# Float64 weights made float32 two chunks at a time: tiles of 2 x 512 columns, two heads' inputs to a tile

## The chip, the cores and the metric

One core of a Trainium2 chip runs the whole program. Its engines each work through a queue of their own in order: TensorE (PE, with its weight loads as PEld), VectorE (DVE), ScalarE (ACT) and GpSimd (POOL); SyncE (SP) issues the DMA transfers. The metric is the device time of one execution in microseconds (us), smaller is better. The kernel before takes 1027.05 us, the median of three runs (1026.56 to 1028.83).

## What is computed

Three layers follow each other: causal attention with a decay bias, and two feed-forward layers without routing, cut to what matters:

```python
# q, k, v: (4, 8, 576, 64)   s: (4, 8, 576)   out: (4 * 576, 512)
def attn(q, k, v, s):
    cum = cumsum(maximum(s, 0), -1)
    scores = q @ k.T / 8 + minimum(-(cum[..., :, None] - cum[..., None, :]), 0)
    p = exp(causal(scores) - rowmax)
    return (p / (p.sum(-1) + 1e-9)) @ v
x = attn(q, k, v, s) as (2304, 512)
h = x @ w1_in               # (512, 2048)
x = (h * clip(h + 3, 0, 6) / 6) @ w1_out
h = x @ w2_in
out = (h * sigmoid(h)) @ w2_out
```

The four weight matrices, of 512 x 2048 or 2048 x 512, are float64: their spreads 1 / sqrt(512) and 1 / sqrt(2048) are float64 scalars by which the float32 draws are multiplied. The chip gets them as pairs of 32-bit words, low word first, and makes float32 values of them with shifts, masks and an addition on integers. The products are then computed with each operand split into a high part (fp32r) and a low part, as high x high + high x low + low x high.

## The kernel before

The attention has 64 heads, 32 of part A (query rows 0 to 255) and 32 of part B (rows 256 to 575), in the order "A0 A1 A2 B0 A3 B1 B2 B3" of part and batch with eight heads each. The first feed-forward layer works on eight blocks of tokens of the same order, each over 16 chunks f of 128 hidden rows; a chunk of the input weights (`W["i", 0, f]`) and one of the output weights (`W["o", 0, f]`) is 128 x 512 values. The second layer works on three blocks of 768 tokens over eight pairs q of chunks.

The loop over slots (L785 on) drives the first part. A slot holds the scores of one head, the second half of the head before it, and, from the tenth slot on, one step of the first layer: `first` (L239 to L241: x times the input weights into the PSUM tile ph), `gate_high` (L251 on ScalarE, L252 on VectorE, then the high part gh) and `gate_low` (L259), and one step later `second` (L278 to L280: into the accumulators acc). In the first block a step is one chunk f, on 256 tokens. The next step's `first` reuses the only ph bank and so needs L252 of the step before.

A chunk of weights (class `Chunk`, L115) lives in one tile of `wpool`, with the tag `i0` to `i15` or `o0` to `o15`. `load` (L132) brings 512 KB of words. `fields` on ScalarE scales the low words (L144) and the high words (L145, into a tile `mag` of the pool `stage`, three buffers). `join` on VectorE is three instructions (L153 sign, L157 shift, L160 addition); `high` (L105, by `copy`) writes the high part into the chunk's own tile, `low` (L171) the low part. `Feed.tick` (L184) takes each chunk through these in turn: load, three ticks later `fields`, one later `join`, one later `high` and `low`. In the trace the tile of the words is rawi or rawo, that of the parts wi or wo, `mag` is magi or mago.

The first feed has the 32 chunks of the first layer. `ticks(3)` (L775) loads three ahead of the slots, between the loads of heads 0 and 1 and the loads of their bias rows (L398, L399); the slots add 0.4 tick each up to the ninth and two each from the tenth (L796). The first 14 heads have their inputs (inA) in the tiles of the chunks that are loaded late (`spare`, L344: one tile to a head); `srow` and `crow` and the rows of `split_rows` lie in tiles `i7`, `o7`, `i15`, `o15`, `i6` and `o6`.

The second layer's input weights go by class `Two` (L843): two chunks at a time are converted with `Chunk`'s instructions, four sums are made of them (L871), and all is split into high and low in a tile w (L881, L883), of which there are two. Its output weights go by a second feed of 16 chunks, ticked by `outs2` (L903): in the last block of the first layer from its ninth step, then twice per pair q. Both take their `mag` tiles from `stage`, and so do three of the four output tiles of `finish1` for the last block (L669).

All this is program order. A scheduler that simulates the engines turns it into the order of each engine's queue: it takes the instruction that stands first in the program among those that are ready at its simulated time. So work is often drawn far ahead, and the order is fixed by the simulated times and not by those on the chip.

Of the kernel before, what the change touches and what calls it, by code (L numbers as in the profile page):

```python
# [27 lines left out]
def kernel(  # L28
# [36 lines left out]
    stage = ctx.enter_context(tc.tile_pool(name="stage", bufs=3))  # L65
# [49 lines left out]
    class Chunk:  # L115
        def __init__(self, kind, m, f):
            self.key = (kind, m, f)
            self.src = ((w1i, w1o), (w2i, w2o))[m][kind == "o"][f]
            self.nm = f"{kind}{m}_{f}"
            self.home = wpool, f"{kind}{f}"  # L120

        def place(self, shape, dt, name):
            pool, tag = self.home
            return pool.tile(shape, dt, tag=tag, name=f"{name}{self.nm}")
# [38 lines left out]
        def high(self, eng):  # L163
            wt = self.place([P, 2, DM], F32R, "w")
            W[self.key] = wt[:, 0, :], wt[:, 1, :]
            copy(eng, W[self.key][0], self.val)

        def low(self, eng):
            hi, lo = W[self.key]
            e = nc.vector if eng == "v" else nc.gpsimd  # L170
            e.tensor_tensor(out=lo, in0=self.val, in1=f32(hi), op=ALU.subtract)  # L171

    class Feed:


        def __init__(self, keys, hi_eng, lo_eng):
            self.ch = [Chunk(*k) for k in keys]
            self.hi_eng, self.lo_eng = hi_eng, lo_eng
# [64 lines left out]
    def gate_high(i):  # L243
# [3 lines left out]
        g = gpool.tile(sh, F32, tag="g", name=f"g{i}")  # L247
# [64 lines left out]
    def bank(kind, shape, name):  # L312
# [7 lines left out]
        wpool.tile([BH, S], F32, tag=f"{kd}{NF // 2 - 1}", name=f"{kd}row") for kd in "io"  # L320
# [7 lines left out]
    def split_rows():  # L328

        def row(tag, name):  # L330
            return wpool.tile([BH, S], F32R, tag=tag, name=name)

        f = NF - 1
        hi, lo = row(f"i{f}", "cumh"), row(f"o{f}", "cuml")
        one, neg = row(f"i{NF // 2 - 2}", "one"), row(f"o{NF // 2 - 2}", "neg")
# [8 lines left out]
    spare = [f"{kd}{f}" for f in range(NF // 2, NF) for kd in "io"][:14]  # L344

    class Head:
# [322 lines left out]
    def finish1(blk, accs):  # L669
        n = sizes[blk][1]  # L670
        per = 512 // n
        for i, c in enumerate(range(0, NDC, per)):
            pool, tag = (gpool, "g") if blk < NB1 - 1 else (stage, "mag") if i else (w7pool, "s4")
            o = pool.tile([P, per, n], F32, tag=tag, name=f"o{blk}_{c}")
# [10 lines left out]
    feed = Feed([(kd, 0, f) for f in range(NF) for kd in "io"], "a", "v")  # L685
# [89 lines left out]
    ticks(3)  # L775
# [8 lines left out]
    for has_head, has_step in plan:  # L784
# [10 lines left out]
        if not feed.done():  # L795
            rate = ((0.4,)*9+(2,))[min(nslot, len(((0.4,)*9+(2,))) - 1)]  # L796
# [98 lines left out]
    feed = Feed([("o", 1, f) for f in range(NF)], "a", "v")  # L895
# [7 lines left out]
    def outs2(upto):  # L903

        while feed.t < min(upto, NF + 5):
# [15 lines left out]
    def split2(b):  # L921
# [5 lines left out]
        def parts(name, x):  # L927
            n0 = 2 + 2 * ["b11", "b22", "t2", "b21", "t3", "t1", "t4"].index(name)
            xh, xl = [
                wpool.tile([P, 2, TH], F32R, tag=f"i{n0 + k}", name=f"x{k}{name}_{b}")  # L930
                for k in range(2)
            ]
# [244 lines left out]
```

## Time and profile before

| | |
|---|---|
| median of 3 runs | 1027.05 us (1026.56 to 1028.83) |
| the profiled execution | 1026.95 us, span 1025.2 us |
| PE busy in the span | 988.9 us (96%) |
| DVE busy | 720.5 us (70%) |
| ACT busy | 523.5 us (51%) |
| chain that ended last | PE 84%, DVE 7%, DMA 5%, SP's queue 3% |
| DMA | 124.78 MB, mean 122 GB/s |

The span is the time from the first to the last instruction of the profiled execution; 1.75 us lie around it. A busy matmul is not one at its peak: its end is modelled and overlaps the next one, so the distance of two starts is the better measure of what one costs. The same holds for instructions that follow each other on VectorE and ScalarE. The chain is followed back from the last instruction to what released each step.

### The profile page before, as it was taken

What the parts mean: (1) busy time and instruction counts of PE and PEld (TensorE: products, weight loads), DVE (VectorE), ACT (ScalarE), POOL (GpSimd) and SP (SyncE); (2) the same over time, 40 slices, a digit from 0 to 9 for tenths busy, and PEclk for the clock granted to TensorE, in tenths of its full rate; (3) what the DMA queues carried; (4) which work ended last, traced back from release to release, by engine and by line L of the source; (5) the groups of instructions that cost most, each with busy time, mean ns of one, the idle gap of its engine ahead of it and who ended that gap; (6) DMA issues with size and microseconds to landing.
All of it is one profiled execution on the core that took longest, in us unless ns stands there. A gap on an engine that the chain in (4) does not pass through costs nothing.

```text
span 1025.2 us, 18219 instructions
## 1 busy us (share of the span) xinstructions
PE 988.9 (96%) x6322; PEld 918.1 (90%) x6322; DVE 720.5 (70%) x1797; ACT 523.5 (51%) x1141; POOL 205.6 (20%) x378
## 2 busy tenths in 40 slices
PE   4978999999999999999999999899999999999997
PEld 3878899999999999999998888789888899888996
DVE  6699996788778887887737997977574343743343
ACT  5697854555455666665515563755353232532232
POOL 5000133443244444444411131000000000000000
PEclk9999999999999999999999999999999999999999
DMA  5794131122312222222113975443345332433411
GB/s 152 208 316 151 49 94 44 51 79 54 90 56 69 85 65 69 86 65 68 58 43 106 350 284 196 143 163 136 144 154 185 144 127 90 165 135 122 144 72 62
DMA packets 52067, 124.78 MB, mean 122 GB/s; under 512 B 10004, under 2 KB 31752, under 8 KB 48648
## 3 DMA queue, kind: packets, MB, share of 16 engines
q1 hardware_dynamic: 51528, 122.97, 35.9%
q8 instruction: 50, 0.82, 0.3%
q10 hardware_dynamic: 448, 0.66, 0.2%
q14 instruction: 41, 0.34, 0.1%
HBM read 98.96 MB, written 24.63 MB: 121 GB/s over the span
## 4 chain that ended last, share of the span: by engine, by line
PE 84%; DVE 7%; DMA 5%; SPq 3%; issue 1%; ACT 1%; DVEq 0%; ACTq 0%
PE ph L239 6%; PE ph L241 6%; PE ph L240 6%; PE acc L279 6%; PE acc L280 6%; PE acc L278 6%; PE a L985 6%; PE a L987 6%; PE a L986 6%; PE h L969 5%; PE h L971 5%; PE h L970 5%; PE poB L595 4%; PE pt0B L546 1%; PE pt1B L546 1%; DMA rawi<-in_w1i_dram 1%
## 5 line engine op out<-in xcount | busy, mean ns | idle before, releaser
L239 PE MATMUL ph<-xh,wi 128*128 128x256 f32 (+1 forms) x512 | 155.0, 304 | 9.0 <-DVE g L252 8.9
L279 PE MATMUL acc<-gl,wo 128*128 128x256 f32 (+1 forms) x512 | 153.2, 301 | 0.8 <-DVE gl L259 0.7
L240 PE MATMUL ph<-xl,wi 128*128 128x256 f32 (+1 forms) x512 | 152.7, 298 | 0.0
L241 PE MATMUL ph<-xh,wi 128*128 128x256 f32 (+1 forms) x512 | 152.4, 298 | 0.0
L280 PE MATMUL acc<-gh,wo 128*128 128x256 f32 (+1 forms) x512 | 151.2, 297 | 0.0
L278 PE MATMUL acc<-gh,wo 128*128 128x256 f32 (+1 forms) x512 | 145.9, 301 | 0.2 <-DVE gh L107 0.2
L1027 ACT ACTIVATE gh<-h 128x384 fp32r<-128x384 f32 x96 | 50.3, 524 | 180.1 <-DVE h L1035 179.8
L985 PE MATMUL a<-wo,gh 128*128 128x512 f32 x288 | 113.0, 392 | 2.2 <-ACT gh L1027 2.2
L986 PE MATMUL a<-wo,gh 128*128 128x512 f32 x288 | 113.0, 392 | 0.0
L239 PEld LDWEIGHTS ph<-xh,wi 128*128 128x128 f32 x512 | 98.0, 192 | 14.0 <-DVE g L252 9.4
L279 PEld LDWEIGHTS acc<-gl,wo 128*128 128x128 f32 x512 | 96.8, 189 | 5.5 <-DVE gl L259 2.2
L240 PEld LDWEIGHTS ph<-xl,wi 128*128 128x128 f32 x512 | 98.3, 192 | 2.9
L241 PEld LDWEIGHTS ph<-xh,wi 128*128 128x128 f32 x512 | 98.1, 192 | 2.8
L280 PEld LDWEIGHTS acc<-gh,wo 128*128 128x128 f32 x512 | 96.6, 189 | 3.7
L278 PEld LDWEIGHTS acc<-gh,wo 128*128 128x128 f32 x512 | 95.8, 189 | 4.5 <-DVE gh L107 0.6
L987 PE MATMUL a<-wo,gl 128*128 128x512 f32 x288 | 89.6, 393 | 0.5 <-DVE gl L1029 0.5
L251 ACT ACTIVATE g<-ph,half 128x512 f32<-128x512 f32 (+1 forms) x80 | 51.3, 644 | 64.7 <-PE ph L241 64.0
L1029 DVE TENSOR_TENSOR gl<-h,gh 128x384 fp32r<-128x384 f32 x96 | 53.4, 556 | 40.6 <-ACT h L1028 38.8
L252 DVE SCALAR_TENSOR_TENSOR g<-g,ph 128x512 f32<-128x512 f32 (+1 forms) x80 | 50.2, 629 | 39.9 <-ACT g L251 39.5
L1035 DVE TENSOR_TENSOR h<-h,u 128x384 f32<-128x384 f32 x72 | 40.1, 557 | 54.0 <-PE h L971 53.7
L99 POOL TENSOR_SCALAR gh<-g 128x512 fp32r<-128x512 f32 x64 | 51.1, 798 | 125.4 <-DVE g L252 113.3
L969 PE MATMUL h<-x0t,w 128*128 128x384 f32 x192 | 65.1, 339 | 0.7 <-DVE u L1035 0.7
(224 smaller groups left out, 2553.3 us busy)
## 6 DMA issues: line engine op xcount, KB each, us to landing
w<-w_d SPq DMA_DIRECT2D x18, 1792.0 KB
w_d<-w SPq DMA_DIRECT2D x8, 1792.0 KB
k2B<-in_kT_dram SPq DMA_DIRECT2D x64, 144.0 KB
rawi<-in_w1i_dram SPq DMA_DIRECT2D x16, 512.0 KB
rawo<-in_w1o_dram SPq DMA_DIRECT2D x16, 512.0 KB
rawi<-in_w2i_dram SPq DMA_DIRECT2D x16, 512.0 KB
rawo<-in_w2o_dram SPq DMA_DIRECT2D x16, 512.0 KB
q2B<-in_qT_dram SPq DMA_DIRECT2D x64, 80.0 KB
```

The lines of the kernel that those rows point to most:

```text
L239: nc.tensor.matmul(o, wih[:, cs], xh[c], start=c == 0, stop=False)
L240: nc.tensor.matmul(o, wih[:, cs], xl[c], start=False, stop=False)
L241: nc.tensor.matmul(o, wil[:, cs], xh[c], start=False, stop=c == NDC - 1)
L251: nc.scalar.activation(g, ph, AF.Relu, bias=half, scale=1.0 / 6.0)
L278: nc.tensor.matmul(a, woh[:, cs], gh[:, jj, :], start=b0, stop=False)
L279: nc.tensor.matmul(a, woh[:, cs], gl[:, jj, :], start=False, stop=False)
L280: nc.tensor.matmul(a, wol[:, cs], gh[:, jj, :], start=False, stop=b1)
L969: nc.tensor.matmul(ps, w[:, 0, cs], xh[:, c, :], start=c == 0, stop=False)
L985: nc.tensor.matmul(accs[t], gh[:, k, cs], woh, start=b0, stop=False)
L986: nc.tensor.matmul(accs[t], gh[:, k, cs], wol, start=False, stop=False)
L987: nc.tensor.matmul(accs[t], gl[:, k, cs], woh, start=False, stop=b1)
L1029: nc.vector.tensor_tensor(out=gl[:, i, o], in0=g, in1=f32(gh[:, i, o]), op=ALU.subtract)
```

## The change

A new class `Pair` replaces `Chunk` in both feeds. A pair is two neighbouring chunks of the same kind in one tile of 2 x 1024 words; its five steps are the same, each as one instruction over 2 x 512 columns, with `high` always on ScalarE. The loads stay one transfer of 512 KB to a chunk. A tick does `join`, `high` and `low` of one pair, then `fields` of the next and the load of a third: load, two ticks later `fields`, one later the rest. `Chunk` stays for `Two`.

The rates become 0.2 and 1 pair to a slot, `ticks(3)` becomes `ticks(2)` (four chunks loaded ahead in place of three), and `outs2` counts in pairs. `stage` has two buffers of 2 x 512 columns in place of three of 512. The pool of gates has two buffers for g and for `finish1`'s outputs in place of three. The first 14 heads lie two to a tile (`shared`), so that such a tile comes free when both its heads are done; the bias rows move to the tiles `i3`, `o7` and `o3` of two chunks. From the fifth pair on, `Two`'s words lie in one tile `i0`. `split2` puts the high and low part of one operand into one tile.

```diff
-    stage = ctx.enter_context(tc.tile_pool(name="stage", bufs=3))
+    stage = ctx.enter_context(tc.tile_pool(name="stage", bufs=2))
...
+    class Pair:
+        def __init__(self, kind, m, j):
+            self.kind, self.m, self.j = kind, m, j
+            src = ((w1i, w1o), (w2i, w2o))[m][kind == "o"]
+            self.src = [src[2 * j + k] for k in range(2)]
...
+        def load(self):
+            raw = self.place([P, 2, 2 * DM], F32 if self.plain else I32, "raw")
+            for k, src in enumerate(self.src):
...
+                    nc.sync.dma_start(raw[:, k, :], src.bitcast(I32))
...
+                words = raw.rearrange("p k (n two) -> p k n two", two=2)
+                self.words = words[:, :, :, 0], words[:, :, :, 1]
+        def fields(self):
+            self.mag = stage.tile([P, 2, DM], I32, tag="mag", name=f"mag{self.nm}")
...
+            nc.scalar.activation(low, low.bitcast(U32), AF.Copy, scale=2.0**-29)
+            nc.scalar.activation(f32(self.mag), f32(high), AF.Abs, scale=2.0**-112)
+        def join(self):
...
+            nc.vector.scalar_tensor_tensor(
+                out=low, in0=high, scalar=SIGN, in1=low,
+                op0=ALU.bitwise_and, op1=ALU.bitwise_or,
+            )
+            nc.vector.tensor_scalar(
+                out=mag, in0=mag, scalar1=3, scalar2=None, op0=ALU.logical_shift_left
+            )
+            nc.vector.tensor_tensor(out=mag, in0=mag, in1=low, op=ALU.add)
+        def high(self):
+            self.wt = self.place([P, 2, 2, DM], F32R, "w")
...
+            nc.scalar.copy(self.wt[:, :, 0, :], f32(self.mag))
...
-            return self.t >= len(self.ch) + 3 + 2
+            return self.t >= len(self.ch) + 2 + 1
...
-            t = self.t - 3
-            lo = self.lo_eng[t % len(self.lo_eng)] if 0 <= t - 2 < n else ""
-            if lo:
-                self.ch[t - 2].high(self.hi_eng[t % len(self.hi_eng)])
+            t = self.t - 2
+            if 0 <= t - 1 < n:
+                self.ch[t - 1].join()
+                self.ch[t - 1].high()
+                self.ch[t - 1].low(self.lo_eng)
             if 0 <= t < n:
                 self.ch[t].fields()
-            if lo == "p":
-                self.ch[t - 2].low(lo)
-            if 0 <= t - 1 < n:
-                self.ch[t - 1].join()
-            if lo == "v":
-                self.ch[t - 2].low(lo)
...
-        g = gpool.tile(sh, F32, tag="g", name=f"g{i}")
+        g = gpool.tile(sh, F32, tag="g", name=f"g{i}", bufs=2)
...
-    spare = [f"{kd}{f}" for f in range(NF // 2, NF) for kd in "io"][:14]
+    spare = [f"{kd}{j}" for j in range(NF // 4, NF // 2) for kd in "io"][:7]
+    shared = {}
...
-                t = wpool.tile([P, 2 * DM], F32, tag=spare[self.at], name=f"in{nm}")
+                j = self.at // 2
+                if j not in shared:
+                    shared[j] = wpool.tile([P, 2, 2 * DM], F32, tag=spare[j], name=f"in{nm}")
+                t = shared[j][:, self.at % 2, :]
...
-    feed = Feed([(kd, 0, f) for f in range(NF) for kd in "io"], "a", "v")
+    feed = Feed([(kd, 0, j) for j in range(NF // 2) for kd in "io"], "v")
...
-    ticks(3)
+    ticks(2)
...
-            rate = ((0.4,)*9+(2,))[min(nslot, len(((0.4,)*9+(2,))) - 1)]
+            rate = 0.2 if nslot <= H else 1.0
...
-                ch.home = (w7pool, f"xr{k}") if q < EARLY else (wpool, f"i{k}")
+                ch.home = (w7pool, f"xr{k}") if q < EARLY else None
         def load(self):
-            for ch in self.ch:
+            if self.q >= EARLY:
+                t = wpool.tile([P, 2, 2 * DM], I32, tag="i0", name=f"raws{self.q}")
+            for k, ch in enumerate(self.ch):
+                if self.q >= EARLY:
+                    ch.home = t[:, k, :]
                 ch.load()
...
-    feed = Feed([("o", 1, f) for f in range(NF)], "a", "v")
+    feed = Feed([("o", 1, j) for j in range(NF // 2)], "v")
...
-        while feed.t < min(upto, NF + 5):
+        while feed.t < min(upto // 2, NF // 2 + 3):
```

## Rows read from the trace of the kernel before

**Rows 1.** The page's busy times, and the shares of the chain that ended last.
```profile
PE 988.9 (96%) x6322; PEld 918.1 (90%) x6322; DVE 720.5 (70%) x1797; ACT 523.5 (51%) x1141; POOL 205.6 (20%) x378
PE 84%; DVE 7%; DMA 5%; SPq 3%; issue 1%; ACT 1%; DVEq 0%; ACTq 0%
```
**Rows 2.** Stretch, length, busy us (instructions) of PE, PEld, DVE, ACT, POOL; clock, DMA.
```profile
12.00:48.00 36.00, 33.90 (x129) 28.85 (x130) 24.66 (x99) 23.11 (x68) 2.07 (x8) 1.00 0.58 167
48.00:150.00 102.00, 89.73 (x647) 83.60 (x647) 99.78 (x297) 78.32 (x185) 12.19 (x25) 0.98 0.48 157
150.00:638.00 488.00, 488.00 (x3679) 467.44 (x3678) 379.26 (x1012) 263.20 (x589) 180.17 (x308) 1.00 0.32 100
638.00:670.00 32.00, 27.89 (x141) 24.76 (x141) 30.62 (x62) 24.41 (x44) 0.00 (x0) 1.00 0.49 171
670.00:1025.00 355.00, 349.23 (x1733) 313.32 (x1731) 180.98 (x324) 129.40 (x251) 0.00 (x0) 1.00 0.36 130
```
**Rows 3.** PE's longest wait from 48 to 150 us: total, times, longest.
```profile
PE ph L239 <- DVE g L252: 8.9, 7, 2.2
```
**Rows 4.** From L251 to the next step: start us, duration us, engine, line.
```profile
67.85 0.48 ACT L251 ACTIVATE g<-ph,half 128x256 f32<-128x256 f32 x1 [0.24 <-PE ph L241]
...
69.44 0.41 DVE L157 TENSOR_SCALAR mago<-mago 128x512 int32<-128x512 int32 x1
69.78 0.68 DVE L153 SCALAR_TENSOR_TENSOR rawo<-rawo 128x512 int32<-128x512 int32 x1
70.38 0.41 DVE L649 TENSOR_TENSOR xl<-xA,xh 128x256 fp32r<-128x256 f32 x1
70.71 0.41 DVE L252 SCALAR_TENSOR_TENSOR g<-g,ph 128x256 f32<-128x256 f32 x1
...
71.18 0.39 PE L239 MATMUL ph<-xh,wi 128*128 128x256 f32 x1 [1.77 <-DVE g L252]
```
**Rows 5.** L171 by stretch: DVE busy us, (x) one for each finished chunk.
```profile
0.00:48.00 48.00, 4.08 (x6) 1.00 0.58 172
48.00:128.00 80.00, 15.68 (x23) 0.98 0.53 177
```
**Rows 6.** PE at the thirteenth step of the first block.
```profile
128.26 0.36 PE L239 MATMUL ph<-xh,wi 128*128 128x256 f32 x1 [0.70 <-DVE g L252]
```
**Rows 7.** L153 by form: count, busy us, mean ns, idle before.
```profile
L153 DVE SCALAR_TENSOR_TENSOR rawi<-rawi 128x512 int32<-128x512 int32 x32 | 21.8, 684 | 4.7 <-ACT rawi L144 4.7
```
**Rows 8.** An instruction of 1024 columns and the next: on VectorE, then on ScalarE.
```profile
566.86 1.21 DVE L883 TENSOR_TENSOR w<-s,w 128x1024 fp32r<-128x1024 f32 x1
567.99 0.68 DVE L160 CUSTOM_DVE_ANT_0 magi<-rawi,magi 128x1024 uint16<-128x1024 uint16 x1
...
684.47 1.05 ACT L881 CAST w<-s 128x1024 fp32r<-128x1024 f32 x1
685.42 0.52 ACT L1028 ACTIVATE h<-h 128x384 f32<-128x384 f32 x1
```
**Rows 9.** The start: second and third chunk on ScalarE, and the first score.
```profile
10.05 0.68 ACT L144 ACTIVATE rawo<-rawo 128x512 int32<-128x512 uint32 x1
...
11.84 0.68 ACT L144 ACTIVATE rawi<-rawi 128x512 int32<-128x512 uint32 x1
...
11.85 0.77 PE L484 MATMUL ps0A<-inA 66*128 66x128 f32 x2 [11.85 <-POOL inA L387]
```
**Rows 10.** Between the layers: PE's two longest waits from 638 to 672 us.
```profile
PE a L985 <- ACT gh L1027: 2.1, 1, 2.1
PE h L969 <- DVE h L1035: 1.5, 1, 1.5
```
**Rows 11.** L145 there, and L171 from 638 to 672 us as in rows 5.
```profile
640.99 1.98 ACT L145 ACTIVATE mago<-rawo 128x512 f32<-128x512 f32 x3 [0.64 <-DMA x2T_d<-o]
...
657.23 0.70 ACT L145 ACTIVATE magi<-rawi 128x512 f32<-128x512 f32 x1 [0.72 <-DVE wo L171]
...
638.00:672.00 34.00, 6.05 (x9) 1.00 0.52 185
```

More of the change, by code (lines that the diff above doesn't have):

```diff
@@ L119, in __init__ @@
             self.nm = f"{kind}{m}_{f}"
[L120 removed]
+            self.home = None
         def place(self, shape, dt, name):
[L123 to L124 removed]
+            if isinstance(self.home, tuple):
+                pool, tag = self.home
+                return pool.tile(shape, dt, tag=tag, name=f"{name}{self.nm}")
+            return self.home[:, : shape[1]].bitcast(dt)
         def load(self):
@@ L161, in join, with place @@
             self.val = f32(mag)
[L163 to L166, printed above, removed]
+    class Pair:
[3 more added lines that the diff above has]
+            self.src = [src[2 * j + k] for k in range(2)]
+            self.plain = src.dtype == F32
+            self.nm = f"{kind}{m}_{j}"
+        def place(self, shape, dt, name):
+            return wpool.tile(shape, dt, tag=f"{self.kind}{self.j}", name=f"{name}{self.nm}")
+        def load(self):
+            raw = self.place([P, 2, 2 * DM], F32 if self.plain else I32, "raw")
+            for k, src in enumerate(self.src):
+                if self.plain:
+                    nc.sync.dma_start(raw[:, k, :DM], src)
+                else:
+                    nc.sync.dma_start(raw[:, k, :], src.bitcast(I32))
+            if self.plain:
+                self.val = raw[:, :, :DM]
+            else:
+                words = raw.rearrange("p k (n two) -> p k n two", two=2)
+                self.words = words[:, :, :, 0], words[:, :, :, 1]
+        def fields(self):
+            self.mag = stage.tile([P, 2, DM], I32, tag="mag", name=f"mag{self.nm}")
+            if self.plain:
+                nc.scalar.copy(f32(self.mag), self.val)
+                return
+            low, high = self.words
+            nc.scalar.activation(low, low.bitcast(U32), AF.Copy, scale=2.0**-29)
+            nc.scalar.activation(f32(self.mag), f32(high), AF.Abs, scale=2.0**-112)
+        def join(self):
+            if self.plain:
+                return
+            low, high = self.words
+            mag = self.mag
+            nc.vector.scalar_tensor_tensor(
[8 more added lines that the diff above has]
+            self.wt = self.place([P, 2, 2, DM], F32R, "w")
+            for k in range(2):
+                W[self.kind, self.m, 2 * self.j + k] = self.wt[:, k, 0, :], self.wt[:, k, 1, :]
+            nc.scalar.copy(self.wt[:, :, 0, :], f32(self.mag))
@@ L168, in low, with __init__ @@
         def low(self, eng):
-            hi, lo = W[self.key]
             e = nc.vector if eng == "v" else nc.gpsimd
-            e.tensor_tensor(out=lo, in0=self.val, in1=f32(hi), op=ALU.subtract)
+            e.tensor_tensor(
+                out=self.wt[:, :, 1, :], in0=f32(self.mag), in1=f32(self.wt[:, :, 0, :]),
+                op=ALU.subtract,
+            )
     class Feed:
-        def __init__(self, keys, hi_eng, lo_eng):
-            self.ch = [Chunk(*k) for k in keys]
-            self.hi_eng, self.lo_eng = hi_eng, lo_eng
+        def __init__(self, keys, lo_eng):
+            self.ch = [Pair(*k) for k in keys]
+            self.lo_eng = lo_eng
@@ L319 @@
     srow, crow = [
-        wpool.tile([BH, S], F32, tag=f"{kd}{NF // 2 - 1}", name=f"{kd}row") for kd in "io"
+        t[:BH, :S]
+        for t in [wpool.tile([P, 2, 2 * DM], F32, tag=f"i{NF // 4 - 1}", name="rows")]
+        for t in (t[:, 0, :], t[:, 1, :])
     ]
@@ L328, in split_rows @@
     def split_rows():
[L330 to L335, printed above, removed]
+        hi, lo, one, neg = [
+            t[:BH, k, :S]
+            for t in [
+                wpool.tile([P, 2, 2 * DM], F32R, tag=f"o{j}", name=f"rows{j}")
+                for j in (NF // 2 - 1, NF // 4 - 1)
+            ]
+            for k in range(2)
+        ]
         nc.gpsimd.memset(f32(one), 1.0)
@@ L673, in finish1 @@
             pool, tag = (gpool, "g") if blk < NB1 - 1 else (stage, "mag") if i else (w7pool, "s4")
-            o = pool.tile([P, per, n], F32, tag=tag, name=f"o{blk}_{c}")
+            o = pool.tile([P, per, n], F32, tag=tag, name=f"o{blk}_{c}", bufs=2 if pool is gpool else None)
             copy("av"[i % 2], o, sums1.pop((blk, c)))
@@ L927, in parts @@
         def parts(name, x):
[L928 to L932, printed above, removed]
+            n = 1 + ["b11", "b22", "t2", "b21", "t3", "t1", "t4"].index(name)
+            both = wpool.tile([P, 2, 2, TH], F32R, tag=f"i{n}", name=f"x{name}_{b}")
+            xh, xl = both[:, 0], both[:, 1]
             nc.scalar.copy(xh, x)
```

## The prediction

> **What bounds the kernel now.** I read the busy times and the chain first: PE is busy for 96% of the span and holds 84% of the chain, DVE 7% [rows 1]. PE's own work is not touched by the change, so only stretches where PE stands still can give anything. The busy times by stage show where these are [rows 2]. From 150 to 638 us PE is busy throughout. From 48 to 150 us it is idle for 102.00 - 89.73 = 12.3 us, while DVE is busy for 99.78 of 102 us. From 638 to 670 us it is idle for 32.00 - 27.89 = 4.1 us, with DVE at 30.62 of 32. From 12 to 48 us it loses 2.1 us with DVE at two thirds, and the 5.8 us after 670 us lie mostly in the tail. So what can be won is some 16 us, in two stretches that DVE fills; the float64 conversion is a large part of DVE's work in both.
>
> PE's waits say how DVE holds it: 8.9 of the 12.3 us are the next step's first matmul waiting for L252, which frees the ph bank [rows 3]. One such wait: L251 ends at 68.33 us, L252 starts only at 70.71, and PE goes on at 71.18 [rows 4]. L252 was ready for 2.4 us and stood behind other instructions of DVE's fixed order, most of them conversion. The weights are not late: at 128 us 29 chunks are done [rows 5], and PE then begins the thirteenth step (f = 12) [rows 6], which needs the 25th. The conversion hurts by filling DVE, not by delivering late.
>
> **The conversion's work.** Four DVE instructions to a chunk become four to a pair. Durations suggest much: 684 ns for 512 columns [rows 7], 1.21 us for 1024 [rows 8]. But instructions overlap, and in a full queue the distance of starts counts: 70.38 - 69.78 = 0.60 us for 512 columns and 69.78 - 69.44 = 0.34 for L157 [rows 4], 567.99 - 566.86 = 1.13 us for 1024 [rows 8]. Two times 0.60 less 1.13 is 0.07 us. L157 has no long form in the trace; its two parts of 0.34 us can save nothing or at most one of them; I give it the same 0.07, from its nearest neighbour. So a pair saves 4 x 0.07 = 0.28 us of 2 x (3 x 0.60 + 0.34) = 4.28, which is 6.5%. Six chunks are done before 48 us [rows 5]; of the other 26, 13 pairs save 3.6 us of DVE's queue in the filled stretch. That is the upper bound by starts. The lower bound is nothing, since PE's own runs lie on the chain there too: only 12.3 of 102 us are waits, and several of these follow from order, not volume. I take 2.0 us off.
>
> [...]
>
> ScalarE has three instructions to a chunk; one of 1024 columns keeps its queue for 685.42 - 684.47 = 0.95 us [rows 8]. ACT is busy for 78.32 of 102 us [rows 2], so what it saves, an estimated 13 x 3 x 0.07 = 2.7 us by DVE's figure, lies beside DVE's work. I count nothing; without DVE as cover it would be that.
>
> **Longer pieces ahead of the gates.** An instruction that becomes ready while DVE works on a conversion waits for what is left of it: half of 0.60 us before, half of 1.13 after, 0.27 us more. L252 and then the following `first` wait for that, once in each of 16 steps of the first block: up to 16 x 0.27 = 4.2 us, and below nothing if the order happens to suit. L252's observed delay of 2.4 us comes from a fixed order, in which what stands ahead counts in whole instructions; half as many conversion instructions can also leave more gaps. I take 0.7 us on.
>
> **The start.** Four chunks are loaded ahead of the bias rows of heads 0 and 1 in place of three. The words of the second and third chunk were taken up 1.8 us apart, and the first score began at 11.85 us, just as the third's were in [rows 9]. A fourth load ahead can put it off by up to 1.8 us; the least is nothing, since SP's total of transfers is unchanged and the next load, now drawn forward, no longer stands among the heads' loads. By 48 us PE has 2.1 us of slack and DVE 11 us [rows 2], and what comes after is set by DVE. I take 0.4 us on. The coarser release of the heads' tiles delays loads by a head at most; with four chunks in hand at 128 us [rows 5, 6] I count nothing, and a head's time if that lead is gone.
>
> **Between the layers.** Before, nine chunks of output weights are finished between 638 and 672 us [rows 11], at 2.14 us of DVE each. Three `mag` tiles are first taken by outputs of the last block, and L145 waits for their DMA to 640.99 [rows 11]. With two `mag` tiles the third output waits for such a DMA itself; its bank is wanted only by the seventh product, so I count nothing, and 640.99 - 638 = 3 us if it blocks DVE. The `mag` tiles of `Two`'s fifth pair are taken from 657.23 on [rows 11] and kept until the split at 684.47 [rows 8]: with only two, no pair of output weights can be converted meanwhile, so about four pairs fit where nine chunks did: 9 x 2.14 = 19.3 us of DVE become 4 x 4.0 = 16.0, and the rest moves behind 684 us, where DVE has room. PE's longest waits there are 2.1 and 1.5 us, both for gates behind DVE [rows 10]. The gain lies between -1 (blocks of 1.13 us ahead of the gates) and 4.1 us; I take 1.5, the second wait, which lies latest. The two g buffers in place of three bite where a block ends and the outputs leave; steps there are over 5 us apart and PE is full [rows 2], so nothing, at most 1 us.
>
> **The sum.** Against the profiled execution's 1026.95 us: -2.0 + 0.7 + 0.4 - 1.5 = -2.4, so 1024.5 us. The execution lies 0.1 us below the median, 1027.05, so the forecast of the one serves for the other. All four terms are small beside their bounds.
>
> **The rivals.** First, the saving is swallowed: the longer pieces cost what the fewer starts save, 3.6 against up to 4.2 us, and the middle gives 0 to 1: 1026 to 1028 us. For it: PE's waits come from order [rows 4]. Against: DVE is full and its volume does fall.
>
> Second, slower: two `mag` tiles make the conversion late. A pair holds its tile over L145, L157, L160, L105 and L171, about 1.0 + 0.6 + 1.1 + 0.95 + 1.1 = 4.8 us, plus five handovers between two crowded engines. Rows 4 show one handover of 2.4 us. At 1.6 us each, two tiles still pass a pair every 6.4 us, which keeps the rate seen before (23 chunks in 80 us [rows 5], 7 us a pair). At 2.4 us each it is 8.4 us a pair: 13 pairs from 48 us end at 157 us, where the last input weights are wanted at about 141, and part of that comes back as PE then waits less for gates. I price it at 3 to 6 us, 1030 to 1033, typically 1031. It decides from a mean handover of about 1.8 us.
>
> Third, more than forecast: durations count, 2 x 0.684 - 1.21 = 0.16 us per merged instruction, 0.63 us a pair, 8.2 us over 13 pairs [rows 7, 8], of which the 12.3 us of waits can take 6, and the middle gives its 1.5 to 2: about 1019 us. [...]
>
> That the change doesn't do what it says would be seen at once in the count of conversion instructions; I give it no chance.
>
> **How the numbers follow.** Forecast 0.42 (own range 1023 to 1026), swallowed 0.25, late conversion 0.20, durations 0.13. What a measurement of this kernel tells from no change is about 0.2%, 2.05 us, so faster begins below 1025.0 and slower above 1029.1. Of the forecast 0.32 lie below and 0.10 within; of the second 0.17 within and 0.08 above; the third is slower, the last faster. Faster 0.45, same 0.27, slower 0.28. The range reaches from the last rival's 1019 to the third's typical 1031.
>
> **What the new profile would show.** L153, L157, L160 and L171 of 1024 or 2048 columns, starts 1.13 us apart in a full DVE queue: the saving by starts. PE's idle time from 48 to 150 us falls from 12.3 to about 11 us, and L252's share of it tells whether the longer pieces hurt. The first score's start tells the fourth load. From 638 to 670 us PE's idle time falls from 4.1 towards 2.6 us, with four pairs finished. Wrong would be PE waiting for wi or wo itself, conversion running past 141 us, or DVE idle for ScalarE's cast between L160 and L171.

## The result, and the profile after

The changed kernel takes 1031.99 us (median, 1031.69 to 1033.28) against 1027.05 us before: a ratio of 1.0055, 95% interval 1.0045 to 1.0066. It is 5 us slower; the forecast was 1024.5. Its profiled execution has a span of 1030.2 us against 1025.2. The page's busy times:

```profile
PE 990.6 (96%) x6322; PEld 920.5 (89%) x6322; DVE 710.4 (69%) x1701; ACT 515.8 (50%) x1069; POOL 202.2 (20%) x378
```

The work fell as it was meant to: DVE from 720.5 to 710.4 us, ACT from 523.5 to 515.8 [rows 1]. So the 5 us are time in which PE stood still or ran slowly. The busy times by stage, with columns as in [rows 2]:

```profile
12.00:48.00 36.00, 34.08 (x130) 29.57 (x130) 25.54 (x90) 23.92 (x65) 2.02 (x6) 1.00 0.49 149
48.00:150.00 102.00, 86.89 (x624) 81.44 (x624) 98.77 (x259) 76.13 (x153) 13.16 (x30) 0.93 0.48 161
150.00:638.00 488.00, 487.83 (x3691) 467.70 (x3690) 369.19 (x979) 256.32 (x565) 175.86 (x303) 1.00 0.30 97
638.00:670.00 32.00, 27.76 (x127) 24.12 (x126) 23.89 (x36) 19.95 (x28) 0.00 (x0) 0.89 0.42 147
670.00:1030.00 360.00, 354.00 (x1758) 317.68 (x1757) 189.45 (x336) 135.46 (x258) 0.00 (x0) 1.00 0.36 134
```

Only two stages differ from before. From 48 to 150 us PE's idle time is 15.1 us in place of 12.3, and the mean granted clock 0.93 in place of 0.98. From 638 to 670 us the idle time is 4.2 us, as it was (4.1), but the clock is 0.89 in place of 1.00. The last step of the first block begins about 5 us later (142.0 against 137.1 us). Some of that is given back, as PE had done other work ahead (725 matmuls by the second block's first step against 704): the second layer's first product begins at 640.27 us against 637.77, and the end comes 5.0 us later. So about half was lost in the first block, half behind 638 us.

**The first block.** PE's waits from 48 to 150 us, in total, times and longest:

```profile
PE poA L669 <- ACT th0A L105: 5.4, 5, 2.3
...
PE ph L290 <- DVE g L303: 2.7, 3, 1.3
```

The wait for the gate (L303, the old L252) fell from 8.9 to 2.7 us [rows 3]. What has come is a wait of the attention for ScalarE's copy th0A. Here is one such wait, first on ScalarE, then on PE (start, duration, engine, line):

```profile
69.20 1.17 ACT L198 ACTIVATE rawo<-rawo 128x1024 int32<-128x1024 uint32 x1 [2.03 <-DMA rawo<-in_w1o_dram]
...
71.55 1.15 ACT L199 ACTIVATE mago<-rawo 128x1024 f32<-128x1024 f32 x1
72.59 1.12 ACT L198 ACTIVATE rawi<-rawi 128x1024 int32<-128x1024 uint32 x1
73.60 0.47 ACT L105 COPY th0A<-pt0A 128x384 f32<-128x384 f32 x1
```
```profile
71.45 0.38 PE L605 MATMUL pt0A<-ident,pb1A 128*128 128x128 f32 x2
74.12 1.54 PE L669 MATMUL poA<-inA,th0A 128*128 128x64 f32 x6 [2.29 <-ACT th0A L105]
```

ScalarE stands 2.03 us for words that are on their way, and all behind it in its queue moves back by as much. PE had finished pt0A by 71.8 us, but its copy has to wait for two more conversion instructions (L199, L198), and PE waits 2.29 us for it. Without the 2.03 us ScalarE would have been through with them by 71.6. ScalarE's waits for words from 40 to 100 us, 6.5 us in all:

```profile
ACT rawo L198 <- DMA rawo<-in_w1o_dram: 3.7, 3, 2.0
...
ACT rawi L198 <- DMA rawi<-in_w1i_dram: 2.8, 4, 1.9
```

Before, the same view has 0.4 us of such waits. But one more was for words, though its row names PE (ScalarE, then PE, in the kernel before):

```profile
93.12 0.67 ACT L144 ACTIVATE rawo<-rawo 128x512 int32<-128x512 uint32 x1 [2.10 <-PE pt0A L546]
```
```profile
95.50 0.39 PE L239 MATMUL ph<-xh,wi 128*128 128x256 f32 x1 [2.14 <-DVE g L252]
```

The load of these words was issued at 89.54 us, and the trace has its last landing event at 93.02, 0.1 us ahead of L144. So it was 2.5 us before, and the mechanism was there already: ph was done at 90.7 us, but the gate's L251 stood behind L144 in ScalarE's queue (93.69 us) and L252 behind L251, so that PE waited 2.14 us.

Why the words are late in the changed kernel shows in the loads' order in SP's queue:

```profile
57.12 0.37 SPq L184 DMA_DIRECT2D rawi<-in_w1i_dram  x1
59.53 0.47 SPq L448 DMA_DIRECT2D q2A<-in_qT_dram  x1
...
60.54 0.33 SPq L184 DMA_DIRECT2D rawi<-in_w1i_dram  x1
...
61.38 0.90 SPq L184 DMA_DIRECT2D rawo<-in_w1o_dram  x2
62.33 1.60 SPq L184 DMA_DIRECT2D rawi<-in_w1i_dram  x2
```

Half of a pair is loaded at 57.12 us. The other half stands behind a head's q2A, which is issued only at 59.53, and then five loads of words are issued from 60.54 to 63.9. The 2.03 us were for the two of rawo at 61.38: their last landing events are at 67.89 and 69.18 us, with the DMA engines 94% busy from 64 to 72 us (below). The loads issued up to 60 us, after and then before:

```profile
rawi<-in_w1i_dram SPq DMA_DIRECT2D x9, 512.0 KB
rawo<-in_w1o_dram SPq DMA_DIRECT2D x8, 512.0 KB
```
```profile
rawi<-in_w1i_dram SPq DMA_DIRECT2D x11, 512.0 KB
rawo<-in_w1o_dram SPq DMA_DIRECT2D x10, 512.0 KB
```

That is 17 chunks against 21, and ScalarE had taken up 14 in both kernels: the lead fell from seven chunks to three, and half a pair is of no use.

**Between the layers.** The last of the four output copies wants a `mag` tile, and so does the next pair's L199 on ScalarE; both tiles hold an earlier output until its transfer lands (VectorE, then ScalarE, then PE):

```profile
645.20 0.69 DVE L107 COPY o<-acc 128x512 f32<-128x512 f32 x1 [2.03 <-DMA x2T_d<-o]
```
```profile
645.89 1.14 ACT L199 ACTIVATE mago<-rawo 128x1024 f32<-128x1024 f32 x1 [3.91 <-DVE o L107]
647.05 1.28 ACT L1088 ACT_TABLE_LOAD   x1
648.35 0.52 ACT L1088 ACTIVATE gh<-h 128x384 fp32r<-128x384 f32 x1
```
```profile
655.63 0.79 PE L1046 MATMUL a<-wo,gh 128*128 128x512 f32 x1 [2.96 <-ACT gh L1088]
656.22 0.63 PE L1047 MATMUL a<-wo,gh 128*128 128x512 f32 x1
656.65 0.63 PE L1046 MATMUL a<-wo,gh 128*128 128x512 f32 x1
...
660.67 0.40 PE L1047 MATMUL a<-wo,gh 128*128 128x512 f32 x1
660.90 0.40 PE L1046 MATMUL a<-wo,gh 128*128 128x512 f32 x1
```

VectorE stands 2.03 us in front of that copy, and ScalarE 3.91 us in front of L199. The row puts ScalarE's wait down to the copy, but the copy's semaphore event (645.904 us) comes after L199's start (645.895), and the transfer of another output has its last landing event at 645.81: ScalarE waits for a transfer as well, not for VectorE. Behind L199 stands the first gate, which comes at 648.35 us (644.85 before). PE still has products to do there and waits only 0.2 us for it. Its wait of 2.96 us is for the third gate (655.07 us), whose sums stand behind conversion in VectorE's queue. Then its matmuls of 512 columns start 0.43 us apart until 660 us, 0.23 us after that.

**The clock.** Stretch, length, PE's busy time, granted clock, DMA share, GB/s:

```profile
64.00:72.00 8.00, 5.23 (x42) 1.00 0.94 356
72.00:81.00 9.00, 6.88 (x34) 0.62 0.82 282
653.00:661.00 8.00, 5.37 (x15) 0.57 0.10 43
```

In each of the two waits shown (2.29 and 2.96 us) the clock falls, and for some 6 to 7 us it lies at 0.50; a third such stretch lies from 56 to 63 us. By windows of 1 us, one less the granted clock times PE's busy time gives what this took: 5.6 us from 48 to 150 us (1.4 before) and 2.5 us between the layers (0 before). It doesn't add up to the microsecond with the idle time; a busy PE there isn't PE at its peak: the matmul at 656.22 us above is busy for 0.63 us, and the next starts 0.43 us after it.

### The profile page after: what moved, and what is told of

It is laid out like the page before. It is cut to its first block, busy times and chain, and to the rows that moved or that the text cites. A ratio compares the mean times of both kernels' runs of the same rounds, so it can differ in the third digit from the quotient of the medians.

```text
span 1030.2 us, 18045 instructions
## 1 busy us (share of the span) xinstructions
PE 990.6 (96%) x6322; PEld 920.5 (89%) x6322; DVE 710.4 (69%) x1701; ACT 515.8 (50%) x1069; POOL 202.2 (20%) x378
## 4 chain that ended last, share of the span: by engine, by line
PE 88%; DMA 3%; DVE 3%; ACT 2%; issue 1%; SPq 1%; POOL 1%; POOLq 0%; DVEq 0%; ACTq 0%
PE ph L290 6%; PE ph L291 6%; PE ph L292 6%; PE a L1046 6%; PE a L1047 6%; PE acc L330 6%; PE acc L329 6%; PE acc L331 6%; PE a L1048 6%; PE h L1030 5%; PE h L1032 5%; PE h L1031 5%; PE poB L654 4%; PE pt0B L605 1%; PE poA L669 1%; PE pt1B L605 1%
## 5 line engine op out<-in xcount | busy, mean ns | idle before, releaser
L303 DVE SCALAR_TENSOR_TENSOR g<-g,ph 128x512 f32<-128x512 f32 (+1 forms) x80 | 50.4, 631 | 47.2 <-ACT g L302 47.0
L99 POOL TENSOR_SCALAR gh<-g 128x512 fp32r<-128x512 f32 x64 | 49.9, 779 | 142.7 <-DVE g L303 129.2
L1030 PE MATMUL h<-xt,w 128*128 128x384 f32 x192 | 65.4, 341 | 0.7 <-DVE u L1096 0.7
```

What stands on the lines that cost most here:

```text
L1030: nc.tensor.matmul(ps, w[:, 0, cs], xh[:, c, :], start=c == 0, stop=False)
```

## The experiments

Each kernel was timed beside the kernel before; the ratio is to that, with its 95% interval, and 1.0055 is the changed kernel's. An edit also moves the fixed order of other work, so that a microsecond or two between two kernels can be order alone; the verdicts therefore go by what the traces show of the cause as well.

**outs: the last outputs two to a tile.**

```diff
+                if i % 2:
+                    both = stage.tile([P, 2, DM], F32, tag="mag", name=f"o{blk}_{c}")
+                o = both[:, 1 - i % 2 : 2 - i % 2, :n]
```

> The changed kernel, but the second to fourth output of finish1's last block lie two to a tile of the pool stage: outputs 1 and 2 in the two halves of one, output 3 in the other, so that no output waits for another one's transfer. Theory (half of the loss is between the layers: VectorE stands 2.0 us at its output copy behind that transfer, and ScalarE behind VectorE): VectorE's copy at about 643 us no longer waits, the first gates come about 3 us earlier, PE's waits for gates there fall from 4.2 us to about 2, and the time is 1029 to 1030 us against 1032.0. Rival (instructions of 1024 columns ahead of the gates make these late, whatever the outputs do): the wait of the copy goes, the gates stay as late, 1031.5 to 1032.5 us.

1.0048 (1.0036 to 1.0060). VectorE's copy no longer waits, but ScalarE's L199 does as it did, for the tile that the outputs hold; here the row names the transfer:

```profile
646.62 1.13 ACT L199 ACTIVATE mago<-rawo 128x1024 f32<-128x1024 f32 x1 [4.04 <-DMA x2T_d<-o]
```

The first gate comes at 649.06 us, as late as ever. The theory's edit failed, as it took away the wait that mattered little: VectorE's 2.03 us by themselves cost nothing that can be told. That the wide pieces are to blame isn't shown either.

**outs_i0: the last outputs in the tile i0, none in `mag`.**

```diff
-            pool, tag = (gpool, "g") if blk < NB1 - 1 else (stage, "mag") if i else (w7pool, "s4")
...
+                if i == 0:
+                    outs = wpool.tile([P, 2, 2 * DM], F32, tag="i0", name="outs")
+                o = outs[:, i // 2 : i // 2 + 1, i % 2 * DM : i % 2 * DM + n]
```

> The changed kernel, but all four outputs of finish1's last block lie in the tile i0, which is free by then, and none in the pool stage. Theory (between the layers the cause is the pool of two mag tiles: whoever takes one there, VectorE's copy or ScalarE's next conversion, stands behind the transfer of the outputs, and the first gates behind it): neither engine waits for that transfer, the first gate comes 3 us earlier against the first product, PE's idle time there falls and its granted clock stays at 1.00; from the first product to the end 387 to 388 us in place of 389.9, 1029 to 1030 us against 1032.0. Rival (the 1024-column instructions ahead of the gates make them late): the wait goes, the gates come as late, the clock falls as before, 1031.5 to 1032.5 us.

0.9985 (0.9975 to 0.9996): 7 us faster than the changed kernel, with the 1024-column instructions in place, and more than I had expected. ScalarE reaches the first gate 3.7 us earlier, and PE has no idle time there at all (ScalarE, then PE by stretch):

```profile
644.68 0.53 ACT L1092 ACTIVATE gh<-h 128x384 fp32r<-128x384 f32 x1 [0.60 <-DVE h L1100]
```
```profile
638.00:653.00 15.00, 15.00 (x78) 1.00 0.79 280
653.00:661.00 8.00, 8.00 (x41) 1.00 0.78 303
```

So it is the outputs in the two `mag` tiles that cost the time between the layers. The gain is the whole of the idle time and clock there (4.4 and 2.5 us from 600 to 680 us), that of the kernel before included. But the edit does more than take a wait away, as the `mag` tiles also come free for conversion earlier. The last instruction of the second feed's pairs (L224) from 640 to 672 us, in the changed kernel and in outs_i0:

```profile
640.00:672.00 32.00, 4.88 (x4) 0.89 0.36 126
```
```profile
640.00:672.00 32.00, 1.22 (x1) 1.00 0.68 246
```

Four pairs are finished in that stretch in the one and one in the other, since before 640 us it is two and five. How much of the 7 us is the wait itself, and how much the conversion that no longer stands among the gates, wasn't separated.

**warm: four matmuls of zeros in the gap.**

```diff
+            if (b, q, k) == (0, 0, 0) and t < 3:
+                for _ in range(2 if t == 0 else 1):
+                    nc.tensor.matmul(accs[t][:, :NZ], ident, cmask[:, :NZ], start=False, stop=False)
```

> The changed kernel with four more matmuls of 128 x 384 zeros on the accumulators of the first output of the second layer, in PE's order just ahead of the matmuls that wait 3.0 us for a gate at 655.6 us; they add nothing to the values and nothing that PE waits for is moved. Theory (half of what is lost between the layers is TensorE's clock: after the idle time the granted clock is 0.50 for some 7 us): with PE occupied in the gap the clock stays at 1.00, and the 5 us of matmuls behind it take half: 1029 to 1030 us against 1032.0. Rival (the fall of the clock costs nothing, as VectorE sets the pace there): clock up, time 1031.5 to 1032.5 us, the matmuls then wait for their gates. Without an effect on the clock: 1032 to 1033.

1.0033 (1.0021 to 1.0045), 2.2 us less than the changed kernel. The gates come as late as there; PE is occupied in the gap, and its clock stays up:

```profile
653.00:661.00 8.00, 7.62 (x33) 1.00 0.16 70
```

With no gate any earlier, the fall of the clock was worth 2.2 us, near the 2.5 counted above.

**lag: a pair loaded one tick earlier, in both feeds.**

```diff
-            t = self.t - 2
+            t = self.t - 3
...
         hd.load_cum()
+    ticks(1)
```

> The changed kernel, but each pair is loaded one tick earlier ahead of its conversion (fields come three ticks after load in place of two, and a third pair is loaded ahead of the slots, behind the bias rows). Theory (the other half of the loss is in the first block: ScalarE waits 6.5 us from 40 to 100 us for words that are still on the way, and the copies of the attention that stand behind in its queue hold PE): ScalarE's waits for words fall below 2 us, PE's wait for L105 (5.4 us) below 3, the second layer begins about 2 us earlier, 1029.5 to 1030.5 us against 1032.0. Rival (the length of the instructions costs, not the transfers): ScalarE's waits for words go and others of the same size come, 1031.5 to 1032.5 us. A second rival: the tiles come free too late for an earlier load (two heads to a tile), the loads move by little and nothing changes.

1.0035 (1.0022 to 1.0048), 2 us less, as the theory wanted. Up to 60 us 19 chunks are issued, in place of 17. ScalarE's waits for words from 40 to 100 us, and PE's for th0A from 48 to 150:

```profile
ACT rawi L198 <- DMA rawi<-in_w1i_dram: 0.6, 1, 0.6
...
ACT rawo L198 <- DMA rawo<-in_w1o_dram: 0.5, 2, 0.3
```
```profile
PE poA L669 <- ACT th0A L105: 1.1, 1, 1.1
```

With one more wait of 0.3 us, whose row names GpSimd although a landing came last, ScalarE's fell from 6.5 to 1.4 us. PE's fell from 5.4 to 1.1 us, the clock from 48 to 150 us is 0.98 again, and the second layer begins at 638.39 us.

**rows: the bias rows ahead of the second pair.**

```diff
-    ticks(2)
+    ticks(1)
     for hd in heads[:loaded]:
         hd.load_cum()
+    ticks(1)
```

> The changed kernel with the bias rows of heads 0 and 1 loaded ahead of the second pair in place of behind it. The first score begins at 11.0 to 11.9 us in place of 13.0. If the start carries through to the end: 1030.8 to 1031.2 us against 1032.0. If it is taken up before the second layer, as the first nine slots have idle time: 1031.7 to 1032.3 us.

1.0038 (1.0025 to 1.0051). The first score begins at 10.36 us in place of 13.0. The gain of 1.7 us isn't simply the start's: with the outputs in i0 the same edit gave almost nothing (rows_i0, below), and with both cures it lost (best_rows). Up to 60 us 19 chunks are issued here, as in lag, so part of the gain may be that of earlier words.

**chunks: the tiles and ticks of the change, instructions of 512 columns.** One of the instructions; the others are cut in two in the same way:

```diff
+            for k in range(2):
+                nc.scalar.copy(self.wt[:, k, 0, :], f32(self.mag[:, k]))
```

> The changed kernel with all its tiles, loads, ticks and buffers, but every conversion instruction of a pair as two of 512 columns. Theory (the tiles and their release cost, the wide instructions themselves give a little): 3 to 4 us more of VectorE's starts by 150 us, the waits for words and for the transfer of the outputs stay; 1032 to 1034 us. Rival (the wide instructions ahead of the gates and of the attention's copies cost the 5 us): 1027 to 1029 us.

1.0080 (1.0067 to 1.0093). The rival falls: without the wide instructions it is 2.6 us slower still. What comes with them (tiles, ticks, buffers) costs 8.2 us against the kernel before, and they give 2.6 of it back. The two places differ: the second layer begins 7.7 us later than in the changed kernel (647.97 us), and the rest takes 4.4 us less, with the clock at 1.00 there.

**narrow2: 512 columns in the second feed alone.** The edit of chunks, for the weights of the second layer.

> The changed kernel with instructions of 512 columns in the second feed alone (the weights of the second layer), tiles, loads and buffers as they are. If the length of the instructions ahead of the gates is what is lost between the layers: PE's waits for gates fall, from the first product to the end 387 us or less, 1029 us or less against 1032.0. If it is the wait for the outputs' transfer: ScalarE or VectorE waits for it as before, the clock falls as before, and VectorE has some 1 us more to do: 1031.5 to 1033 us.

1.0039 (1.0024 to 1.0054). Inconclusive, and partly unexpected: PE's clock from 638 to 670 us stays at 1.00, and the time is 1.6 us less than the changed kernel's. The second layer begins 3.3 us later (643.54 us), and the rest takes 4.3 us less. The order of the last block differs too much to tell the length of the pieces from that.

**all: the outputs in i0, the bias rows first, and the earlier loads in both feeds.**

> The changed kernel with three edits together: the outputs in the tile i0, the bias rows ahead of the second pair's load, and each pair loaded one tick earlier ahead of its conversion. If the three causes (outputs' transfer, late first score, late words) are separate and add up: 1032.0 less 2.5, 1.5 and 2.0, about 1026 us, level with the kernel before or a little faster. If the two edits at the start take up the same idle time: 1027.5 to 1028.5 us.

1.0003 (0.9993 to 1.0013), 1.8 us slower than outs_i0 alone: the three edits don't add up. From 48 to 150 us the clock falls three times again (4.9 us lost). Even so the second layer begins 1.2 us earlier than in outs_i0 (639.37 us); the rest takes 2.3 us more, which isn't explained.

**i0_lag1: the outputs in i0, the earlier loads in the first feed alone.**

> The changed kernel with the outputs in i0, and in the first feed alone each pair loaded one tick earlier ahead of its conversion, a third pair behind the bias rows. If the two causes are separate: first product at 638.4 us, as in the kernel with the earlier loads, and 382.8 us from there to the end, as in the one with the outputs in i0: 1022.5 to 1023.5 us. If the first block's loss comes from elsewhere and was only moved by a new order: first product at 639.5 us or later, 1024.5 us or more.

0.9960 (0.9948 to 0.9972), 1022.9 us: 9 to 10 us less than the changed kernel, 4.1 less than the kernel before, and the fastest of all. The two causes are separate and add up: the second layer begins at 638.28 us, as in lag, and takes 382.8 us from there, as in outs_i0. PE is busy throughout behind 638 us:

```profile
638.00:670.00 32.00, 32.00 (x164) 1.00 0.68 246
```

**rows_i0: the outputs in i0, the bias rows first.**

> The changed kernel with the outputs in i0 and the bias rows of heads 0 and 1 ahead of the second pair's load. If the earlier first score (10.4 us) carries through: first product at 638.9 us, then 382.8 us, 1023 to 1024 us. If it is taken up in the first block (the steps there wait for VectorE and ScalarE all the same): 1025 us.

0.9981 (0.9969 to 0.9994), not to be told from outs_i0's 0.9985. The second layer begins 1.9 us earlier (638.63 against 640.56 us), but the rest takes 1.2 us more. So no cost of the late start can be told at the end; what it is worth by itself isn't settled.

**best_rows: i0_lag1 with the bias rows first.**

> The changed kernel with the outputs in i0, each pair of the first feed loaded one tick earlier, and the bias rows ahead of the second pair's load. If the first score at 10.5 us in place of 13.3 carries through: 1020.5 to 1021.5 us. If the first block takes it up: 1022.5 to 1023.5 us.

0.9984 (0.9973 to 0.9995), 2.5 us slower than without. The score's earlier start (10.57 us) is lost in the first block, where the clock takes 4.7 us in place of 1.6: the second layer begins no earlier (638.65 us). Behind that it takes 1.8 us more, with 1.1 us of idle time of PE that i0_lag1 doesn't have. That a good edit in one place costs in another is the fixed order's doing here, not explained further.

**before_i0: the kernel before, with its outputs in i0 and i1.**

> The kernel before with the outputs of finish1's last block in the tiles i0 and i1 and none in the pool stage. It tells whether the outputs in mag tiles cost the old kernel too. If they do (its L145 waits for that transfer to 640.99 us, and PE has 4.1 us of idle time from 638 to 670 us): from the first product to the end 383 to 385 us in place of 387.4, 1022.5 to 1025 us against 1027.0; the change is then still 1 to 3 us slower than this. If three mag tiles hide it: 1026.5 to 1027.5 us, and the changed kernel with its outputs in i0 (1025.3) is the gain that the change has without this fault.

1.0038 (1.0026 to 1.0050): slower, which neither side expected. ScalarE now stands before the first gate for words, and the gate comes at 649.29 us in place of 644.85:

```profile
646.25 0.66 ACT L144 ACTIVATE rawi<-rawi 128x512 int32<-128x512 uint32 x1 [3.09 <-issue]
...
649.29 0.52 ACT L1031 ACTIVATE gh<-h 128x384 fp32r<-128x384 f32 x1
```

The row names no releaser for the 3.09 us. The load of these words, issued only at 642.74 us, has its last landing event at 646.17, and it had waited in SP's queue for the outputs, since the words of `Two`'s fifth pair go to the tiles i0 and i1 that the outputs now hold:

```profile
SPq L132 <- DMA x2T_d<-outs: 3.7, 2, 3.5
```

So the tiles weren't free here, and it is the same wait for the outputs by another way. In outs_i0 the fifth pair's load waits for them too, but its conversion stands behind the first three gates (651.41 us). What decides is what stands ahead of the first gate in ScalarE's queue, and there the two kernels have different orders.

**before_lag: the kernel before, chunks loaded two ticks earlier.**

> The kernel before with each chunk of the first feed loaded two ticks earlier ahead of its conversion (five ticks in place of three, two more chunks behind the bias rows). If late words are a fault of the change alone (ScalarE waits 0.4 us for words from 40 to 100 us before, 6.5 us after): 1026.5 to 1027.5 us, no gain. If more lead helps the kernel before as well: 1024.5 to 1025.5 us.

1.0019 (1.0009 to 1.0029): no gain, slightly a loss. The edit did little of what it should: up to 60 us 21 chunks are issued, as before, and ScalarE's waits for words fell from 2.5 us (the 0.4 of the expectation is short of the 2.10 shown above) to 1.7. PE's idle time from 48 to 150 us fell from 12.3 to 8.8 us, but the clock takes 4.7 in place of 1.4. So the run doesn't show that late words came only with the change.

**narrow1_i0 and narrow2_i0: outs_i0 with 512 columns in one feed. best_narrow: i0_lag1 with 512 columns in both.**

> The changed kernel with the outputs in i0 (1025.3 us), and instructions of 512 columns in the first feed alone. By the starts, 16 pairs x 0.28 = 4.5 us more on VectorE by 140 us, of which 2 to 4 reach the end as PE waits for VectorE there: 1027 to 1029 us. If the wide instructions' gain lies in the second feed alone (there the narrow ones cost 5 us): 1025 to 1026 us.

> The changed kernel with the outputs in i0 and instructions of 512 columns in the second feed. With the wait for the transfer gone, it tells what the 1024-column instructions are worth between the layers by themselves. If VectorE's volume or the length of its pieces mattered there: 1 us or more away from 1025.3 us, with PE's idle time from 638 to 675 us other than 0. If neither does, as PE then has no idle time there: 1025 to 1026 us.

> The changed kernel with the outputs in i0 and each pair of the first feed loaded one tick earlier (1022.9 us), but with every conversion instruction of a pair as two of 512 columns. If the wide instructions save what their starts say (0.28 us a pair, 13 pairs in the filled stretch, 3.6 us at most) and as much between the layers: 1025 to 1029 us. If only the tiles and the order matter: 1022.5 to 1024 us. Slower than 1029 us: the narrow instructions cost more than their starts, in order or in what shares their time.

1.0036 (1.0024 to 1.0048), 1.0041 (1.0027 to 1.0055) and 1.0066 (1.0054 to 1.0078). Against their wide counterparts (0.9985, 0.9985 and 0.9960) the narrow instructions cost 5.2, 5.7 and 10.9 us: some 5 us in each feed, and with the outputs in i0 the two add up; with the outputs in `mag` it was 2.6 us for both (chunks) and a gain for the second alone (narrow2). For the second feed the expectation had left open 1 us or more, or nothing. By the starts 16 pairs are 16 x 0.28 = 4.5 us in the first feed and 8 pairs 2.2 in the second, so starts alone don't explain the second. Part of it is a wait that the wide kernel doesn't have (GpSimd, then PE, in narrow2_i0):

```profile
634.56 3.37 POOL L99 TENSOR_SCALAR gh<-g 128x512 fp32r<-128x512 f32 x1 [5.54 <-DVE g L309]
```
```profile
637.98 1.20 PE L335 MATMUL acc<-gh,wo 128*128 128x512 f32 x4 [2.71 <-POOL gh L99]
```

In the first feed the clock has a share as well: from 48 to 150 us it is 0.85 in narrow1_i0 and 0.97 in outs_i0, which by the count under "The clock" above is 13.7 against 3.1 us lost. How these parts divide wasn't settled.

## Why the prediction was wrong

**The saving by starts, -2.0: right in kind, its size not settled.** In the changed kernel the starts stand as the working had them, and L211, for which I had only a neighbour, at 0.60:

```profile
654.85 1.22 DVE L214 CUSTOM_DVE_ANT_0 mago<-rawo,mago 128x2048 uint16<-128x2048 uint16 x1
655.98 0.55 DVE L1096 TENSOR_TENSOR h<-h,u 128x384 f32<-128x384 f32 x1
656.45 0.69 DVE L211 TENSOR_SCALAR mago<-mago 128x1024 int32<-128x1024 int32 x1
657.05 0.56 DVE L1090 TENSOR_TENSOR gl<-h,gh 128x384 fp32r<-128x384 f32 x1
```

1.13 and 0.60 against twice 0.60 and 0.34 [rows 4]: 3 x 0.07 + 0.08 = 0.29 us a pair. The wide instructions were worth 5.2 us in the first feed (narrow1_i0), where I took 2.0 of 3.6. That is more than all their starts there (16 x 0.29 = 4.6 us), and the clock differs by more than that between the two runs, so how much of VectorE's saving reaches the end isn't shown. The durations, with the third rival's 0.63 us a pair, would give 16 x 0.63 = 10 us there; the starts show half of it.

**The longer pieces, +0.7: wrong.** The gate's wait fell from 8.9 to 2.7 us, which by itself says nothing of the length, as with 512 columns it is as short (0.2 us in narrow1_i0, 2.3 in best_narrow). But in each run with 512 columns in the first feed the second block begins later than with 1024: 152.8 against 146.7 us (chunks, changed kernel), 151.4 against 147.4 (narrow1_i0, outs_i0), 149.9 against 142.5 (best_narrow, i0_lag1). In the first and the last of these the clock takes about the same (6.1 and 5.6, 1.6 and 1.6 us).

**The coarser release and the loads, counted at nothing: the first step that failed.** I read the lead where PE takes the finished weights, as ample, and misread that too: the matmuls at 128.26 us [rows 6] are the fourteenth step (f = 13), since the first step's lie scattered, so the lead there was two chunks and not four. What mattered lies elsewhere: the words' lead at ScalarE, whose queue is in order and holds the attention's copies as well. It fell from seven chunks to three. The price was 2.0 us (lag) to 2.5 us (i0_lag1 against outs_i0). The text's own condition, "a head's time if that lead is gone", was the right question, put to the wrong queue. "The weights are not late" was wrong for the kernel before as well: one of its seven waits for L252, 2.14 of the 8.9 us, goes back to words that ScalarE stood for. How much of the lead went to pairs that load as one, and how much to two heads in a tile, wasn't tried by itself.

**Between the layers, -1.5: the second step that failed.** I had seen that an output would wait for a transfer, wrote "3 us if it blocks DVE", and took nothing, since PE wants that accumulator's bank late. But it isn't that copy which holds the gates (outs took its wait away, and the first gate came no earlier): the next pair's L199 wants a `mag` tile too and stands 3.91 us for a transfer, in ScalarE's queue, ahead of the first gate. Four pairs are finished in the stretch, as forecast, and some of their instructions stand ahead of the sums of the later gates. The cost was about 7 us against what the same kernel can do there, and 2.5 us against the kernel before, which had lost 4.1 us at that place.

**The clock had no term.** All waits were priced at their own length, though [rows 2] has 0.98 from 48 to 150 us. Before, two waits of 2.1 and 1.5 us [rows 10] left the clock at 1.00; here one of 2.96 cost another 2.2 to 2.5 us behind it (warm).

**The start, +0.4.** The first score came 1.1 us later (12.97 against 11.85 us [rows 9]), within the bound, and at the end no cost of it can be told (rows_i0).

**The rivals.** The first, the saving swallowed by longer pieces, isn't what the runs show: in the first feed the longer pieces were the better ones. The second, slower, named the time (1030 to 1033 us, typically 1031) but not the mechanism: the conversion isn't late. Its last instruction ends at 129.1 us, before at 133.0. Two `mag` tiles did cost, though not by handovers: by outputs that sat in them. The third, 0.16 us a merged instruction, isn't seen in the starts. The range ended at 1031, 1 us short, because it took the later conversion at its middle.

## What to carry to other kernels

Where work is merged into larger units, price what the unit takes with it: the load that must be complete, the buffer count, the release. Look for it in every in-order queue that holds the merged work, not only in the engine that should gain; a wait costs what stands behind it there. A buffer that waits for an outgoing transfer shouldn't come from the pool that feeds the critical engines, nor be a tile that the next loads want (before_i0). A row names one releaser: where the engine named has nothing to do with the waiting instruction, look when the transfer landed. And a wait of PE is priced only when the granted clock of the stretch behind it has been read too.

## What the runs showed of the hardware

The clock's fall can cost nearly as much as the wait: PE's matmuls of 512 columns start 0.43 us apart behind the gap at 655 us, at a granted clock of 0.50, and 0.23 us once it is back at 1.00, and four matmuls of zeros in the gap, which bring nothing forward, made the kernel 2.2 us faster, where the wait itself was 2.96 us.

GpSimd's copy of a gate's high part (L99, 128 x 512) has a median of 0.62 us in the changed kernel, but beside a gapless VectorE it took up to 6.41 us, in outs_i0:

```profile
613.93 6.41 POOL L99 TENSOR_SCALAR gh<-g 128x512 fp32r<-128x512 f32 x1 [0.28 <-DVE g L303]
```

VectorE ran seven instructions from 613.70 to 619.86 us without a gap, and the copy ended, at 620.34 us, only when VectorE stood still and waited 0.51 us for it. What holds the copy up no run here shows (spans on GpSimd are rough).
